# Nyström attention with two expert layers on one core: the second head group is placed in reversed partition order, eight heads' products go to the matrix array in one run, and G is made batch by batch

## The chip, the cores and the metric

The kernel runs on one core of a Trainium2 chip. Its engines work side by side, each through its own list of instructions in order: TensorE (matrix products; PE in the rows, with PEld for its weight loads), VectorE (DVE), ScalarE (ACT), GpSimd (POOL) and SyncE (SP), which here only starts DMA transfers. The metric is the device time of the whole kernel in microseconds (us), lower is better.

## The reference, cut to what matters

```
A = sm(q, k_lm);  Bm = sm(q_lm, k_lm);  C = sm(q_lm, k)     # 8 batches, 8 heads, S = 576, D = 64, 32 landmarks
Z = six steps of  Z = 2 Z - Z @ Bm @ Z                      # per head, 32 x 32
attn = A @ Z @ C @ v                                        # x = attn as (4608, 512)
x = relu(x @ w_in) ** 2 @ w_out                             # 512 -> 2048 -> 512, for every token
out = one of 8 experts for every token (relu(x @ w1) @ w2, scaled), picked by argmax(x @ w_gate)
```

All inputs are fp32. The kernel joins the end of the attention with the first layer: for each batch it makes W = Z C v (per head 32 x 64) and G = W @ w_in (32 rows of landmarks of each of 8 heads against 2048 columns), so that `x @ w_in` becomes `A @ G` with 256 rows to sum over instead of 512.

## The kernel before, in words

**Three stages.** A prologue loads q, k, v of batch 0, makes its attention parts and converts w_in and w_out. Then `gemm(b)` runs for the eight batches, each in two halves of 288 tokens (`c`): six matmuls (L998, tile `hp`) make 128 of the 2048 columns of `A @ G`, ScalarE and VectorE square them and split them into a high and a low part (L1009 to L1012), and twelve matmuls (L1045, tile `acc`) multiply by w_out, two steps later. Last, `experts` runs the expert layers (L1234, L1260).

**Side work.** While `gemm` of one batch runs, the attention of later batches is fed in small steps: `point()` is called between its matmuls and takes a share of a step (`RATE`) from `all_steps`, which weaves the `unit` of one batch with the G steps of the one before. `settle(b)` makes sure that G of batch b is there before `gemm(b)`. All of it is given to a list scheduler that fixes each engine's order when the kernel is built; a smaller priority number goes first among what it takes to be ready, and `high_priority(n)` lowers the number by n.

**Heads in the array.** The eight heads are two groups of four (`hg`), a group has its 32 landmarks of each head in 32 of the 128 partitions: head h in `32*h`. So scores (`scores_a`, `scores_c`) of a group and a half are four matmuls of a 64 x 32 weight tile and 288 columns, each into its own 32 partitions of one PSUM bank, and the same four column strips serve both groups. Batches 0 and 1 (`pe`) have q and k transposed by TensorE, with a half c in rows 64c to 64c+63 for all four heads; from batch 2 on VectorE transposes (`flipped`), and heads 0 and 1 lie in rows 0 to 63, heads 2 and 3 in rows 64 to 127.

**G.** W is written twice side by side with a mask (`hm`, L636), transposed, and is then block-diagonal with zeros: `wt[:, hg, p2]`, 128 rows (two heads) by 64 columns. Batch 0 makes G in `first_g_of` (L827) with w_in still in SBUF. Batches 1 to 3 make it alone (`g_alone`): 16 matmuls of 128 x 64 weights and 512 columns in fp32, two by two into the halves of a bank. Batches 4 and 5, and 6 and 7, make it together (`GROUPS`, `g_steps`): 48 matmuls of 128 x 128 weights and 512 columns in fp32r for two batches, for which ScalarE and GpSimd split each piece of w_in into two parts (L188, L191, tile `wi`). w_in comes back from DRAM (`win_d`) each time, in 16 pieces of 256 KB. A result goes from its bank by a ScalarE copy to `gs` and by DMA to `g_d`, from which `load_g` fetches it for `gemm`.

**Banks.** After the first G, side work has one pool of three PSUM banks (`aux`) for everything it makes; `hp` has one, `acc` four.

## Time and profile before

| | |
|---|---|
| time, median of 3 runs | 1343.86 us (1340.45 to 1346.6) |
| profiled execution: time, span | 1345.73 us, 1344.0 us |
| granted TensorE clock, mean | 0.977 of full |
| busy: PE, PEld, DVE, ACT, POOL | 95%, 83%, 59%, 47%, 29% |
| chain that ended last | PE 72%, DVE 13%, DMA 6%, issue 3%, ACT 3%, POOL 2% |
| DMA | 172.38 MB, mean 128 GB/s |

The span is the time from the first to the last instruction of the one execution that was profiled. Busy shares are of that span; matmuls overlap in the engine, so a run of them counts as one stretch from the first start to the last end. The chain is followed back from the last instruction, at each step to what released it.

### The profile page before, as it was taken

The numbers are of one execution on the slowest core, as the hardware profiler recorded it, in microseconds if no ns is written. First come the engines' busy times: TensorE is split into PE (matmuls) and PEld (weight loads), VectorE is DVE, ScalarE is ACT, GpSimd is POOL, SyncE is SP. The second block draws the span as 40 slices with busy tenths as digits, with TensorE's granted clock in tenths as the row PEclk, the third lists the DMA queues.
The fourth block names the chain that finished last, engine by engine and source line by source line (L and its number), as shares of the span: only waits on it lengthen the run. The fifth ranks groups of instructions, "written<-read, shape, count | busy, mean of one in ns | idle before, by whom it ended". The sixth has DMA issues, their size and how long they took to land.

```text
span 1344.0 us, 25108 instructions
## 1 busy us (share of the span) xinstructions
PE 1273.1 (95%) x9458; PEld 1111.6 (83%) x9458; DVE 787.0 (59%) x1760; ACT 628.6 (47%) x1385; POOL 383.6 (29%) x305
## 2 busy tenths in 40 slices
PE   6588999999999999999999999999999999999996
PEld 3267868688788888898989999998898888888885
DVE  7999968669769897787653433454423233233231
ACT  5576454455535557545654344444434334334231
POOL 3556222113013134313622112024323323323210
PEclk8688999999999999999999999999999999999998
DMA  9866283462723237613652112014345344353321
GB/s 325 272 202 184 84 279 100 170 199 77 228 63 108 82 119 210 179 62 95 207 144 67 42 35 67 1 54 140 100 129 152 100 141 134 98 157 93 106 91 37
DMA packets 126683, 172.38 MB, mean 128 GB/s; under 512 B 10558, under 2 KB 84062, under 8 KB 126558
## 3 DMA queue, kind: packets, MB, share of 16 engines
q1 hardware_dynamic: 126078, 170.18, 41.4%
q8 instruction: 76, 1.25, 0.4%
q10 hardware_dynamic: 384, 0.52, 0.1%
q14 instruction: 49, 0.40, 0.1%
q0 software_dynamic: 96, 0.03, 0.0%
HBM read 128.19 MB, written 42.51 MB: 127 GB/s over the span
## 4 chain that ended last, share of the span: by engine, by line
PE 72%; DVE 13%; DMA 6%; issue 3%; ACT 3%; POOL 2%; SPq 1%; DVEq 0%; POOLq 0%; ACTq 0%
PE acc L1045 22%; PE hp L1234 15%; PE y L1260 13%; PE hp L998 11%; PE bank L346 6%; PE y L1271 2%; DVE g L1010 2%; DVE gl L1012 2%; DVE sums L382 2%; DMA raw<-in_moe_w_in_dram 1%; PE pl L1072 1%; DMA g<-gs 1%; DMA gr<-g 1%; DVE x L413 1%; DMA w<-win 1%
## 5 line engine op out<-in xcount | busy, mean ns | idle before, releaser
L1045 PE MATMUL acc<-gh,wo 128*128 128x288 f32 x2048 | 456.6, 299 | 2.7 <-DVE wo L191 2.4
L1045 PEld LDWEIGHTS acc<-gh,wo 128*128 128x128 f32 x2048 | 342.9, 189 | 25.8 <-issue 16.0
L1045 PE MATMUL acc<-gl,wo 128*128 128x288 f32 x1024 | 288.8, 301 | 9.4 <-DVE gl L1012 9.0
L998 PE MATMUL hp<-ab,gb 128*128 128x288 f32 x1536 | 255.9, 302 | 1.3 <-ACT r L1009 0.5
L1010 DVE TENSOR_TENSOR g<-r 128x288 f32<-128x288 f32 x256 | 145.9, 571 | 162.8 <-ACT r L1009 162.1
L998 PEld LDWEIGHTS hp<-ab,gb 128*128 128x128 f32 x1536 | 219.0, 190 | 22.0 <-issue 6.9
L1009 ACT ACTIVATE r<-hp 128x288 f32<-128x288 f32 x256 | 105.3, 412 | 242.3 <-PE hp L998 237.8
L1234 PEld LDWEIGHTS hp<-xs,s 128*128 128x128 f32 x1536 | 210.7, 188 | 8.9 <-issue 0.9
L1234 PE MATMUL hp<-xs,s 128*128 128x288 f32 x1536 | 215.5, 295 | 0.0
L1045 PEld LDWEIGHTS acc<-gl,wo 128*128 128x128 f32 x1024 | 193.9, 189 | 21.8 <-DVE gl L1012 15.6
L1260 PE MATMUL y<-s,h 128*128 128x512 f32 x768 | 190.6, 396 | 0.0
L1260 PEld LDWEIGHTS y<-s,h 128*128 128x128 f32 x768 | 141.3, 188 | 29.2
L1012 DVE TENSOR_TENSOR gl<-g,gh 128x288 fp32r<-128x288 f32 x256 | 144.9, 566 | 25.9 <-ACT gh L1011 8.2
L191 POOL TENSOR_TENSOR s<-r,s 128x512 fp32r<-128x512 f32 x64 | 83.2, 1300 | 245.5 <-ACT s L188 241.6
L191 DVE TENSOR_TENSOR s<-r,s 128x512 fp32r<-128x512 f32 x64 | 51.5, 805 | 152.2 <-ACT s L188 152.1
L191 POOL TENSOR_TENSOR gb<-gr,gb 128x512 fp32r<-128x512 f32 x56 | 74.4, 1330 | 225.3 <-ACT gb L188 118.0
L188 ACT CAST s<-r 128x512 fp32r<-128x512 f32 x128 | 78.6, 617 | 116.2 <-PE y L1271 91.8
L1243 DVE SCALAR_TENSOR_TENSOR h<-hp,h 128x64 fp32r<-128x64 f32 (+2 forms) x192 | 62.7, 355 | 113.1 <-ACT h L1240 113.0
L1011 ACT ACTIVATE gh<-r 128x288 fp32r<-128x288 f32 x256 | 114.1, 446 | 6.6
L1240 ACT ACTIVATE h<-hp 128x288 fp32r<-128x288 f32 x128 | 52.5, 411 | 134.3 <-PE hp L1234 125.4
L382 DVE TENSOR_REDUCE sums<-t 128x32 f32<-128x576 f32 x64 | 71.2, 1165 | 10.1 <-DMA t<-in_q_dram 5.6
L191 POOL TENSOR_TENSOR xs<-xr,xs 128x1152 fp32r<-128x1152 f32 x16 | 45.7, 2862 | 68.4 <-ACT xs L188 63.2
(193 smaller groups left out, 1327.2 us busy)
## 6 DMA issues: line engine op xcount, KB each, us to landing
r<-in_moe_w_dram SPq DMA_DIRECT2D x128, 256.0 KB
w<-win SPq DMA_DIRECT2D x80, 256.0 KB
gr<-g SPq DMA_DIRECT2D x56, 256.0 KB
t<-in_k_dram SPq DMA_DIRECT2D x16, 576.0 KB
t<-in_q_dram SPq DMA_DIRECT2D x16, 576.0 KB
v<-in_v_dram SPq DMA_DIRECT2D x48, 192.0 KB
x_d<-x SPq DMA_DIRECT2D x16, 576.0 KB
xr<-x_d SPq DMA_DIRECT2D x16, 576.0 KB
```

Source lines behind the costliest of these rows:

```text
L188: hi = self.nc.scalar.copy(out=t[:, 0], in_=raw)
L191: (lo_eng or self.nc.gpsimd).tensor_tensor(out=t[:, 1], in0=raw, in1=t[:, 0].bitcast(F32), op=ALU.subtract)
L346: self.last_pe = self.nc.tensor.matmul(out, **kw)
L382: self.nc.vector.tensor_reduce(out=s[:, 0, ds], in_=t[:, :, ds].rearrange("p s d -> p d s"), axis=AX.X, op=ALU.add)
L998: mm = nc.tensor.matmul(hp[:, 0:HC], lhsT=g[:, l, hg, fs], rhs=at[:, r, hg, :], start=(i == 0), stop=(i == 5))
L1009: nc.scalar.activation(out=r, in_=hp[:, 0:HC], func=ACTF.Relu, scale=1.0 / 256)
L1010: nc.vector.tensor_tensor(out=g2, in0=r, in1=r, op=ALU.mult)
L1011: nc.scalar.activation(out=gh, in_=r, func=ACTF.Square)
L1012: nc.vector.tensor_tensor(out=gl, in0=g2, in1=gh.bitcast(F32), op=ALU.subtract)
L1045: nc.tensor.matmul(acc[m][:, 0:HC], lhsT=self.wo[f][:, l, ms], rhs=r, start=(f == 0 and i == 0), stop=(f == NFC - 1 and i == 2),)
L1234: nc.tensor.matmul(hp[:, 0:HC], lhsT=s1[:, l, kk, :], rhs=xs[j, c][:, r, kk, :], start=(k == 0), stop=(k == 3 * KD - 1),)
L1260: nc.tensor.matmul(acc[t], lhsT=l, rhs=s2[:, r, :], start=(first and k == 0), stop=(last and k == 2))
```

## The change: what it does

1. `place_of`: in the second head group head h lies in partitions `32*(3-h)`, everywhere (scores, softmax B, C v, W, G). A head of the first group and one of the second that share the 64 rows of the array then stand in different column strips.
2. From batch 2 on `scores` issues both groups of a half: eight matmuls into two banks, the second group first, at a priority raised by 300 (`TOGETHER`). Batches 0 and 1 keep four at a time.
3. W is no longer masked: it is written twice by the last addition itself (`hm` and L636 go), and after the transpose each head's 64 x 32 weights stand twice, in rows 0 to 63 and 64 to 127.
4. G is made for one batch at a time, in fp32: `g_part` issues eight matmuls of 64 x 32 weights and 512 columns for 512 of the 2048 columns, into two banks, with the same raised priority. So 32 matmuls of a batch stand where 16 (128 x 64, fp32) or 24 (128 x 128, fp32r) stood. The splits of w_in (L188 and L191 with `wi`) and the low part of W (L662) go.
5. w_in is kept in `win_d` as four pieces of 1 MB and fetched by 28 DMAs of 1 MB (before: 80 of 256 KB); two pieces are held, and piece n + 2 is fetched once the matmuls on n are done. G is stored by DMAs of 512 KB (before 256 KB, or 128 KB).

```diff
-GROUPS = [(0,), (1,), (2,), (3,), (4, 5), (6, 7)]
+LAST = 6
+TOGETHER = 300
...
+def place_of(hg, h):
+    i = 3 - h if hg else h
+    return slice(32 * i, 32 * i + 32)
...
-    def scores_a(self, u, hg, c):
...
-        sa = self.bank()
-        for h in range(4):
-            p, x = self.columns(u, "q", hg, h, c)
-            self.matmul(sa[32 * h:32 * h + 32, 0:HC], lhsT=u["kl"][p, hg, h, :], rhs=x, start=True, stop=True)
...
+    def scores(self, u, lm, nm, groups, c):
+        banks = {hg: self.bank() for hg in groups}
+        with self.tc.high_priority(TOGETHER):
+            for hg, h in itertools.product(reversed(groups), range(4)):
+                p, x = self.columns(u, nm, hg, h, c)
+                self.matmul(
+                    banks[hg][place_of(hg, h), 0:HC], lhsT=u[lm + "l"][p, hg, h, :], rhs=x, start=True, stop=True
+                )
+        return banks
+
+    def parts_of(self, u):
+        return [((hg,), c) for hg in range(2) for c in range(2)] if u["pe"] else [((0, 1), c) for c in range(2)]
...
+        if i == 6:
+            wb = u["wb"] = sm.tile([128, 2, 2, D], F32, tag="ks", name="wb", bufs=1)
+            twice = [128, 2, 2, D]
+            nc.vector.tensor_tensor(
+                out=wb, in0=was[:, :, LM:].unsqueeze(2).to_broadcast(twice),
+                in1=pp[:, :, LM:].unsqueeze(2).to_broadcast(twice), op=ALU.add,
+            )
+            return
...
+        u["wt"] = self.wtp.tile([128, 2, 128], F32, tag="wt", name="wt", bufs=2)
+        nc.scalar.copy(out=u["wt"].rearrange("p g x -> p (g x)"), in_=pw[:, 0:256])
...
+    def g_part(self, wt, w):
+        pg = [self.bank(), self.bank()]
+        with self.tc.high_priority(TOGETHER):
+            for hg, h in itertools.product((1, 0), range(4)):
+                p, at = slice(64 * (h % 2), 64 * (h % 2) + 64), place_of(hg, h)
+                self.matmul(pg[hg][at], lhsT=wt[p, hg, at], rhs=w[2 * hg + h // 2][p], start=True, stop=True)
+        return pg
...
+    def g_steps(self, u):
...
+        def fetch(n):
+            if n < 4:
+                raws[n] = self.wi.tile([128, KD, 512], F32, tag="wi", name="w")
+                nc.sync.dma_start(out=raws[n], in_=self.win_d[n])
+
+        for n in range(2):
+            fetch(n)
+        for _ in range(4):
             yield STEP
...
+        for n in range(4):
+            w = raws.pop(n)
+            pg = self.g_part(u["wt"], [w[:, k] for k in range(KD)])
+            fetch(n + 2)
+            gs = self.gs.tile([128, 2, 512], F32, tag="gs", name="gs")
+            for hg in range(2):
+                nc.scalar.copy(out=gs[:, hg], in_=pg[hg])
+            self.put_g(u["b"], n, gs)
+            for _ in range(4):
                 yield STEP
```

What the scheduler makes of it, at the places that the prediction speaks of. First TensorE at G of batch 2, before (a row is a run of like instructions; `w,wt` are G's matmuls):

```order
L346 MATMUL bank<-w,wt_2917 64x512 x6
L998 MATMUL hp<-ab,gb 128x288 x6
L1045 MATMUL acc<-gh,wo 128x288 x4
L349 MATMUL bank<-ident,sums 128x128 x2
L1045 MATMUL acc<-gl,wo 128x288
```

and with the change, the same place and, 22 rows on, the third piece of w_in:

```order
L349 MATMUL bank<-w,wt 32x512 x12
L935 MATMUL hp<-ab,gb 128x288 x6
L982 MATMUL acc<-gh,wo 128x288 x4
L349 MATMUL bank<-w,wt 32x512 x4
L982 MATMUL acc<-gl,wo 128x288
```
```order
L982 MATMUL acc<-gh,wo 128x288
L349 MATMUL bank<-x,lm 32x288 x8
L349 MATMUL bank<-w,wt 32x512 x4
L935 MATMUL hp<-ab,gb 128x288 x6
L982 MATMUL acc<-gh,wo 128x288
```

Before, pairs of G matmuls stood in runs of two, four or six; now the eight of a piece stand in one run where both banks were free in the schedule (the first run of twelve is piece 0 and half of piece 1), and otherwise as two runs of four. Over batches 1 to 7 these 224 matmuls make 45 sets that can stand in the array at once (7 runs of eight, 4 runs of twelve that are a set of eight and one of four, 30 sets of four or what a shorter run breaks off).

Second, TensorE at the second kind of scores (`scores_a`) of batch 2 with the change (`x,lm` are the scores' matmuls), where the first half's two groups stand apart and the second half's eight together:

```order
L982 MATMUL acc<-gh,wo 128x288
L349 MATMUL bank<-x,lm 32x288 x4
L349 MATMUL bank<-bc,dg 128x96
L935 MATMUL hp<-ab,gb 128x288 x6
L982 MATMUL acc<-gh,wo 128x288 x4
```
```order
L982 MATMUL acc<-gh,wo 128x288
L349 MATMUL bank<-eu,dg 128x96
L349 MATMUL bank<-x,lm 32x288 x8
L349 MATMUL bank<-eu,dg 128x96
L935 MATMUL hp<-ab,gb 128x288 x6
```

Before, batches 2 to 7 have 48 groups of four there; with the change 16 runs of eight and 16 groups of four.

Third, SyncE's list at G of batch 2 with the change (`win_108` is w_in's third piece, `win_109` the fourth, `win_106` and `win_107` the first two, for the next batch):

```order
L367 DMA t<-in_q_dram 128x1152
L367 DMA t<-in_k_dram 128x1152
L860 DMA w<-win_108 128x2048
L848 DMA g_0_134<-gs 128x1024
L860 DMA w<-win_109 128x2048
L848 DMA g_1_135<-gs 128x1024
L882 DMA gr<-g_0_134 128x2x256 x2
L860 DMA w<-win_106 128x2048
```

The first two pieces of a batch are fetched a batch ahead; the third and the fourth are fetched while the first two are used, behind two loads of q and k.

## Rows read from the trace of the kernel before

**Rows 1.** Busy time of the engines in stretches of the span: stretch (us), its length, then busy us (and instructions) of PE, PEld, DVE, ACT and POOL, the granted TensorE clock, the DMA engines' share and GB/s.

```profile
50.00:62.00 12.00, 8.05 (x42) 3.39 (x42) 11.82 (x18) 7.35 (x15) 8.49 (x9) 0.62 0.91 294
205.00:266.00 61.00, 59.00 (x465) 47.83 (x465) 46.11 (x106) 26.73 (x62) 12.88 (x13) 1.00 0.38 121
430.00:483.00 53.00, 52.85 (x523) 47.07 (x522) 47.13 (x125) 28.83 (x71) 9.39 (x9) 1.00 0.23 69
483.00:547.00 64.00, 61.10 (x478) 53.10 (x477) 49.65 (x89) 41.13 (x93) 29.27 (x26) 1.00 0.68 202
648.00:704.00 56.00, 54.26 (x374) 50.17 (x373) 31.34 (x67) 31.81 (x71) 22.80 (x17) 1.00 0.59 169
744.00:912.00 168.00, 167.18 (x1217) 157.74 (x1216) 74.73 (x185) 68.93 (x159) 25.62 (x18) 1.00 0.14 41
912.00:1344.00 432.00, 419.45 (x2478) 373.21 (x2476) 135.43 (x312) 153.84 (x294) 120.22 (x77) 0.99 0.39 114
```

**Rows 2.** Groups of TensorE's matmuls by form, for scores (`x,lm`) and G (the other three): busy us, mean ns of one record, then the idle time ahead of them and what ended it. An fp32 matmul leaves two records, an fp32r one leaves one.

```profile
L346 PE MATMUL bank<-x,lm 64*32 64x288 f32 x512 | 46.0, 442 | 2.7 <-DVE gb L837 1.3 <-ACT gs L934 0.9 <-ACT lm L447 0.5
L346 PE MATMUL bank<-wi,wt 128*128 128x512 f32 x96 | 28.7, 404 | 1.3 <-ACT wi L188 1.0 <-DVE wt L662 0.3
L346 PE MATMUL bank<-w,wt 128*64 128x512 f32 x96 | 28.4, 614 | 1.3 <-DMA w<-win 1.3
L827 PE MATMUL bank<-wf,wt 128*64 128x512 f32 x32 | 10.8, 797 | 1.1 <-ACT wt L660 0.6 <-ACT x L398 0.4
```

**Rows 3.** Scores in TensorE's order of time (start us, length us, records): one group of four heads of batch 3, and three groups in a row of batch 5, each with the row behind it.

```profile
260.97 0.69 PE L346 MATMUL bank<-x,lm 64*32 64x288 f32 x8
261.59 0.40 PE L1045 MATMUL acc<-gl,wo 128*128 128x288 f32 x1
...
434.96 1.66 PE L346 MATMUL bank<-x,lm 64*32 64x288 f32 x24
436.55 0.40 PE L1045 MATMUL acc<-gh,wo 128*128 128x288 f32 x1
```

**Rows 4.** The scores' records alone in two stretches of the same length, with the records that started in them: stretch, length, PE busy us (records), granted clock, DMA share and GB/s. The first is of batch 1, two groups behind each other that read rows 0 to 63 and rows 64 to 127; the second is of batch 5.

```profile
86.10:86.56 0.46, 0.42 (x16) 1.00 0.31 125
434.90:435.36 0.46, 0.40 (x8) 1.00 0.00 0
```

**Rows 5.** The run of batch 1 of which rows 4 show a part, in order of time.

```profile
86.14 0.72 PE L346 MATMUL bank<-x,lm 64*32 64x288 f32 x16
```

**Rows 6.** G of batches 1 to 3 in order of time: a set of two matmuls (batch 3) and a run of six (batch 2), each with the row behind it.

```profile
343.02 1.08 PE L346 MATMUL bank<-w,wt 128*64 128x512 f32 x4
344.03 0.44 PE L349 MATMUL bank<-ident,sums 128*128 128x128 f32 x2
...
246.78 2.80 PE L346 MATMUL bank<-w,wt 128*64 128x512 f32 x12
249.51 1.06 PE L998 MATMUL hp<-ab,gb 128*128 128x288 f32 x6
```

**Rows 7.** G of batches 6 and 7 in order of time: a run of nine matmuls and the row behind it.

```profile
656.74 2.26 PE L346 MATMUL bank<-wi,wt 128*128 128x512 f32 x9
658.84 0.96 PE L998 MATMUL hp<-ab,gb 128*128 128x288 f32 x6
```

**Rows 8.** Waits at G, in order of time: in brackets the idle us ahead of the row and what ended it.

```profile
254.95 1.04 PE L346 MATMUL bank<-w,wt 128*64 128x512 f32 x2 [1.34 <-DMA w<-win]
514.20 0.69 PE L346 MATMUL bank<-x,lm 64*32 64x288 f32 x8 [0.92 <-ACT gs L934]
687.96 0.50 PE L346 MATMUL bank<-wi,wt 128*128 128x512 f32 x1 [1.04 <-ACT wi L188]
```

**Rows 9.** The chain that ended last, at G of batch 2 (start us, us, what): 512 KB of w_in in two DMAs.

```profile
248.80 6.02 DMA w<-win
254.81 0.14 issue
```

**Rows 10.** The engines in the stretch of rows 9, columns as in rows 1.

```profile
249.00:262.00 13.00, 11.52 (x72) 8.01 (x68) 7.17 (x12) 4.94 (x12) 0.80 (x2) 1.00 0.92 325
```

**Rows 11.** The first G (batch 0) in order of time, and what follows it.

```profile
55.26 5.56 PE L827 MATMUL bank<-wf,wt 128*64 128x512 f32 x16 [0.55 <-ACT wt L660]
60.75 0.55 PE L349 MATMUL bank<-ident,t 128*128 128x128 f32 x3
```

**Rows 12.** Groups on VectorE, ScalarE and GpSimd that the change removes or touches (columns as in rows 2).

```profile
L636 DVE TENSOR_TENSOR wb<-eu,hm 128x256 f32<-128x256 f32 x8 | 3.3, 416 | 0.1
L662 DVE TENSOR_TENSOR wt<-bank,wt 128x256 fp32r<-128x256 f32 x4 | 1.7, 421 | 0.9 <-ACT wt L660 0.9
L837 DVE TENSOR_TENSOR gb<-bank,gb 128x256 fp32r<-128x256 f32 x16 | 6.2, 412 | 0.7 <-ACT gb L834 0.7
L461 DVE STREAM_TRANSPOSE aa<-bank 128x288 f32<-128x288 f32 x32 | 15.1, 472 | 3.0 <-PE bank L346 2.9
L188 ACT CAST wi<-w 128x512 fp32r<-128x512 f32 x32 | 19.6, 620 | 3.1 <-DMA w<-win 2.8 <-POOL wi L191 0.3
L934 ACT COPY gs<-bank 128x512 f32<-128x512 f32 x32 | 18.7, 584 | 16.7 <-DMA g<-gs 12.9 <-PE bank L346 3.3
L191 POOL TENSOR_TENSOR wi<-w,wi 128x512 fp32r<-128x512 f32 x32 | 42.8, 1346 | 35.7 <-ACT wi L188 31.7 <-PE bank L346 3.9
```

More of the change, by code (lines that the diff above doesn't have):

```diff
@@ L204, in job @@
                 place,
[L205 removed]
+                lambda w: self.nc.sync.dma_start(out=self.win_d[n][:, kp], in_=w),
             )
@@ L280, in run @@
             stage = self.experts(jobs)
-            for b in GROUPS[-1]:
+            for b in range(LAST, B):
                 self.gemm(b, last=stage)
@@ L302, in constants @@
         make_identity(nc, ident)
-        self.win_d = {
-            (n, k): drm.tile([128, 512], F32, name=f"win_{n}_{k}") for n in range(4) for k in range(KD)
-        }
+        self.win_d = [drm.tile([128, KD, 512], F32, name=f"win_{n}") for n in range(4)]
         self.at_d = [[drm.tile([128, S], F32, name=f"at_{b}_{g}") for g in range(2)] for b in range(B)]
@@ L478, in softmax_a, with scores_c @@
         yield STEP
-    def scores_c(self, u, hg, c):
+    def scores_c(self, u, groups, c):
         nc = self.nc
-        if hg == c == 0:
+        if groups[0] == c == 0:
             u["mc"] = self.sm.tile([128, 2, 8], F32, tag="mc", name="mc")
             u["ec"] = self.wk.tile([128, 2, S], F32, tag="ec", name="ec")
-        sc = self.bank()
-        for h in range(4):
-            p, x = self.columns(u, "k", hg, h, c)
-            self.matmul(sc[32 * h:32 * h + 32, 0:HC], lhsT=u["ql"][p, hg, h, :], rhs=x, start=True, stop=True)
-        to, src = u["ec"][:, hg], sc[:, 0:HC]
-        if u["pe"]:
-            to = to.rearrange("p (r c i l) -> p c i r l", c=2, i=3, l=LM)[:, c]
-            src = src.rearrange("p (i r l) -> p i r l", i=3, l=LM)
-        else:
-            to = to[:, c * HC:(c + 1) * HC]
-        nc.scalar.copy(out=to, in_=src)
-        nc.vector.tensor_reduce(out=u["mc"][:, hg, c:c + 1], in_=sc[:, 0:HC], axis=AX.X, op=ALU.max)
-        if c == 1:
+        for hg, sc in self.scores(u, "q", "k", groups, c).items():
+            to, src = u["ec"][:, hg], sc[:, 0:HC]
+            if u["pe"]:
+                to = to.rearrange("p (r c i l) -> p c i r l", c=2, i=3, l=LM)[:, c]
+                src = src.rearrange("p (i r l) -> p i r l", i=3, l=LM)
+            else:
+                to = to[:, c * HC:(c + 1) * HC]
+            nc.scalar.copy(out=to, in_=src)
+            nc.vector.tensor_reduce(out=u["mc"][:, hg, c:c + 1], in_=sc[:, 0:HC], axis=AX.X, op=ALU.max)
+        for hg in groups if c == 1 else ():
             mc, ec = u["mc"][:, hg], u["ec"][:, hg]
@@ L699, in unit @@
             yield STEP
-        for hg in range(2):
-            for c in range(2):
-                self.scores_c(u, hg, c)
-                yield STEP
+        for hg, c in self.parts_of(u):
+            self.scores_c(u, hg, c)
+            yield STEP
         def cv():
@@ L756, in sooner, with unit_of @@
             yield STEP
-    def unit_of(self, b, bi, wt, early=None):
-        return dict(b=b, bi=bi, wt=wt, early=early, pe=b < PE_BATCHES)
-    def weights_of(self, parts):
-        made = []
-        def get():
-            if not made:
-                made.extend(
-                    self.wtp.tile([128, 2, 2, 2, 64], F32R if parts == 2 else F32, tag=f"wt{j}", name=f"wt{j}")
-                    for j in range(parts)
-                )
-            return made
-        return get
+    def unit_of(self, b, early=None):
+        return dict(b=b, early=early, pe=b < PE_BATCHES)
     def prologue(self, right):
@@ L839, in all_steps @@
     def all_steps(self):
         g = iter(())
-        for group in GROUPS[1:]:
-            wt = self.weights_of(len(group))
-            for bi, b in enumerate(group):
-                yield from weave(self.unit(self.unit_of(b, bi, wt)), g)
-            g = self.g_steps(group, wt)
-        yield from g
-    def put_g(self, group, hg, n, gs, rows):
-        def store():
-            for bi, b in enumerate(group):
-                self.nc.sync.dma_start(
-                    out=self.g_d[b][n][rows, hg, :], in_=gs[64 * bi:64 * bi + 64] if len(group) == 2 else gs
-                )
-        self.after(2, store)
-        if hg == 1 and rows.stop == 128:
-            self.after(3, lambda: self.have.update((b, n) for b in group))
```

138 lines of the change are left out of this document (29 added, 109 removed).

## The prediction

> **What bounds the kernel now.** I read the stretches first. From 205 us on TensorE is busy nearly all the time (59.0 of 61 us, 52.85 of 53, 61.1 of 64, 167.2 of 168), at the full clock [rows 1]. So a microsecond taken off TensorE's work between about 150 and 704 us is worth a microsecond, as long as nothing else comes up behind it. What could is VectorE: 47.1 of 53 us at 430 to 483 [rows 1]. Before 62 us it is the other way round: VectorE is busy 11.8 of 12 us, TensorE 8.1, at a clock of 0.62. From 744 us on there is no side work, and the change has nothing there: 600 of the 1344 us stay.
>
> Next the groups by form: scores and G are what the change touches [rows 2]. Then their places in order of time, for what one set takes away from `gemm`: the distance from its start to the start of the next matmul, since the last record is drawn out beyond that.
>
> **Scores.** A group of four takes 0.62 us (260.97 to 261.59), and three in a row take 1.59 [rows 3], so 0.49 for a further one: a set on its own pays some 0.13 us for going to the small tiles and back. Do eight stand side by side? Batch 1 shows it without the change: two groups behind each other, one on rows 0 to 63 and one on rows 64 to 127, in the same four column strips and in two banks. In 0.46 us 16 records start, where in batch 5 only eight do [rows 4], and the whole run of 16 is drawn 0.72 us long against 0.69 for eight [rows 5, 3]. So eight cost 0.65 us instead of 0.62 + 0.62 apart. The order shows that only 16 of the 24 pairs came to stand together. Before: 48 x 0.62 less two runs of three (0.26 each) = 29.2 us. After: 16 x 0.65 + 16 x 0.62 = 20.3 us. That is **-8.9 us**.
>
> The Trainium skill ("TensorEngine Tiling (Array Packing)", Restrictions and Gotchas) says that different row tiles cannot use the same PSUM bank at the same time. By that, a group of four with heads in both row halves of one bank would go in two turns, and every set of the new G, which has both halves in each bank, too. The trace disagrees for sets in different partitions of the bank: batch 5 has its heads 0 and 1 in the upper and 2 and 3 in the lower rows, in one bank, and its eight records start within 0.46 us [rows 4].
>
> **G.** Before, batches 1 to 3: a set of two matmuls takes 1.01 us, three sets 2.73 [rows 6]; the group's 28.4 us [rows 2] less the 0.07 by which the last record of each of its 24 runs is drawn out (1.08 against 1.01) gives 26.7. Batches 4 to 7: nine fp32r matmuls take 2.10 us, 0.233 each [rows 7], times 96 = 22.4. Together 49.1 us. After, no row shows four or eight matmuls of 64 x 32 with 512 columns. A set streams the same 512 columns as the sets of two, in fp32, and four or eight narrow scores took no longer than fewer of them, so I take 1.01 for four, 1.05 for eight, 1.9 for twelve. The bounds: at best 0.85 (a further set in the run of six: (2.73 - 1.01)/2), at worst the eight go as two fours, 1.9. The 45 sets of the order: 30 x 1.01 + 7 x 1.05 + 4 x 1.9 = 45.3, less 0.13 for the ten that stand right beside scores = 44.0 us: **-5.1 us**. Had all 28 eights come together it would be 29, -20 us; the two banks that were not free in the schedule cost most of what G could give.
>
> **The old waits at G.** 1.34 for w_in, 0.92 for a bank whose `gs` copy was late, 1.04 for a split [rows 8]. The places are gone in this form: **-3.3 us**. The copies, which waited 12.9 us for their stores [rows 12], remain.
>
> **New waits for w_in.** Piece 2 of a batch is fetched when piece 0 has been used. Between the two stand, in batch 2, 12 `hp` and 24 `acc` matmuls at 0.138 each (168 us for 1217 [rows 1]), half of piece 1, four small transposes and one run of scores: 5.0 + 1.0 + 0.4 + 0.65 = 7.1 us. By the same count it is 7 to 8 us in batches 1, 2, 4, 6 and 7, 11 in batch 5 and 16 in batch 3; piece 3 has 16 to 20 (6 in batch 7). Now 512 KB took 6.0 us from issue to use at that very place [rows 9], where the DMA engines were busy 0.92 and moved 325 GB/s [rows 10]. Another 512 KB is 1.6 us more: 7.6. With one more load of q or k (576 KB, 1.8 us) ahead it is 9.4. So a wait of 0 to 2.3 us in five batches; the nearest row is itself a wait, so I take 1 us in each: **+5 us**. TensorE is in order: all of `gemm` stands behind that wait. Bounds 0 and +12.
>
> **Two banks at once.** A run of eight needs two of the three banks free when it comes up; what is behind it on TensorE waits too. Emptying one is 0.47 us on VectorE or 0.58 on ScalarE [rows 12]. All the waits ahead of scores and G sum to 5.3 us now [rows 2], mostly named above. Below: nothing. Above: half of the 52 places (24 pairs of scores, 28 pieces of G) wait for one copy, 26 x 0.5 = 13. Nearest to what is there: **+2 us**.
>
> **The first G.** 16 records took 5.5 us (55.26 to 60.75) at the low clock [rows 11]. As two sets of eight they would take 3.5. But behind them are the copies and 16 subtractions of 0.41 us [rows 12] on a VectorE that is nearly full there [rows 1]. Bounds 0 and -2, I take **-1 us**.
>
> **Costed at nothing.** The mask (L636, 8 x 0.42) and the low part (L662, 4 x 0.42) lie on VectorE beside `gemm`; the splits of w_in are 19.6 us of ScalarE and 42.8 of GpSimd [rows 12]. The stretches with the splits, less the 11 us of G in each, are no longer than others, so they hardly delay TensorE; were the cover gone, a split that TensorE waits for is 1 us [rows 8]. 28 MB of w_in instead of 20 MB is 26 us of DMA at 325 GB/s, in stretches where the DMA engines are mostly idle; it shows only as the wait priced above. G by batch also lets batch 4's G come before unit 5; `gemm(4)` has no wait of its own in the rows.
>
> **Sum.** The profiled execution took 1345.7 us. -8.9 -5.1 -3.3 +5 +2 -1 = -11.3 gives 1334.4. It stands 1.9 above the median of the runs, so the median should come to **1332.5 us**, call it 1332.
>
> **Rivals.**
> *More comes out (about 1319).* Pieces land in time, banks are free, the first G counts in full: +5 and +2 become 0, -1 becomes -2, and without splits and with fewer changes of tile size some 5 us of other waits go too. For it: GpSimd and ScalarE lose 62 us in the stretches where `gemm` runs slowest (64 and 56 us). Against: the DMA was full at G.
> *The waits take the gain (about 1342).* w_in +9, banks +7 instead of 5 and 2: 1332.5 + 9. For it: the raised priority puts each set at the first moment that the schedule thinks possible, so whatever is later in fact is a wait of TensorE.
> *Slower (about 1355).* The 1 MB pieces. If loads of q, k and w_in and the stores of G queue up so that the 14 pieces 2 and 3 are waited for 2 us each on the mean, in place of 5 us in all: 1332.5 - 5 + 28. It decides from 1.2 us a piece on (then the time is that of before), and from 1.7 us it is half a percent slower. For it: 0.92 busy [rows 10]; against: mean use is 69 to 202 GB/s [rows 1], and piece 3 has 16 us.
> *Eight do not stand together with 512 columns, or only as fours.* Then each eight of G costs 1.9: 11 x 0.85 = +9, about 1342; rows 4 speak against it.
> *By the rule on row tiles and banks*, each set of G would go in two turns: 45 x 0.85 = +38, and scores would not gain: about 1379. Rows 4 show the opposite for 288 columns.
>
> **Chances.** Forecast (1325 to 1337) 0.50, more 0.18, waits 0.18, no eights 0.04, slower 0.08, the rule 0.02. Half a percent is 6.7 us, about what a measurement of this kernel can tell: faster (under 1337) 0.68, same 0.23, slower 0.09. The range takes in the better rival and the waits: 1317 to 1346.
>
> **What would show it.** Right: `x,lm` records in runs of 16 drawn about 0.7 us long; `w,wt` runs of eight records about 1.08 us and of 16 about 1.1, under a name with 64 rows by 32 columns; their busy sum near 48 against 57.1 us; `gemm(6)`, which starts the stretch at 744, about 11 us earlier; from there on the same 600 us. Waits for `w<-win` ahead of piece 2, around 1 us. Wrong: G records in two turns (1.9 us for 16); idle time of TensorE behind `gs` copies or `w<-win` above 10 us in sum; VectorE at over 95% of a stretch while TensorE idles; or a start of `gemm(0)` that moved by several us, since the order of the prologue moved too.

## The result, and the profile after

The changed kernel takes 1364.38 us (median of 4 runs, 1357.15 to 1366.31) against 1343.6 for the kernel before in the same session: a ratio of 1.0148, 95% interval 1.0115 to 1.0181. It is slower by 21 us where 11 us of gain were forecast. The profiled execution took 1364.93 us with a span of 1363.2 and a mean clock of 0.963.

**The priced terms held.** TensorE's groups by form, columns as in [rows 2]:

```profile
L982 PE MATMUL acc<-gh,wo 128*128 128x288 f32 x2048 | 466.0, 303 | 5.2 <-ACT wo L196 2.7 <-ACT gh L948 2.1 <-DVE wo L199 0.3
L982 PE MATMUL acc<-gl,wo 128*128 128x288 f32 x1024 | 294.9, 304 | 16.0 <-DVE gl L949 15.7
L935 PE MATMUL hp<-ab,gb 128*128 128x288 f32 x1536 | 262.7, 307 | 13.6 <-ACT r L946 9.1 <-DVE gb L826 4.4
L349 PE MATMUL bank<-w,wt 64*32 64x512 f32 x448 | 48.1, 600 | 3.1 <-DMA w<-win 3.1
L349 PE MATMUL bank<-x,lm 64*32 64x288 f32 x512 | 37.1, 445 | 2.3 <-ACT et L587 1.3 <-DVE mc L512 0.5 <-ACT lm L450 0.5
```

Scores went from 46.0 to 37.1 us, G from 28.7 + 28.4 to 48.1, and the waits for w_in are 3.1 us. What is new stands in the other three groups, which are `gemm`'s own: TensorE waits 9.1 us for `r` and 15.7 for `gl`. The same two groups before:

```profile
L1045 PE MATMUL acc<-gl,wo 128*128 128x288 f32 x1024 | 288.8, 301 | 9.4 <-DVE gl L1012 9.0
L998 PE MATMUL hp<-ab,gb 128*128 128x288 f32 x1536 | 255.9, 302 | 1.3 <-ACT r L1009 0.5 <-DVE gb L837 0.5
```

The sets took what was forecast (1.01, 1.05 and 1.9). In order of time, a set of four matmuls of G (8 records), one of eight (16) and a run of twelve (24), each with the row behind it, answering [rows 6]:

```profile
259.85 1.06 PE L349 MATMUL bank<-w,wt 64*32 64x512 f32 x8
260.84 0.40 PE L982 MATMUL acc<-gl,wo 128*128 128x288 f32 x1
...
524.05 1.09 PE L349 MATMUL bank<-w,wt 64*32 64x512 f32 x16
525.07 0.69 PE L1009 MATMUL pl<-x,wg 128*32 128x288 f32 x8
...
256.48 1.92 PE L349 MATMUL bank<-w,wt 64*32 64x512 f32 x24
258.33 1.06 PE L935 MATMUL hp<-ab,gb 128*128 128x288 f32 x6
```

From start to start they take 0.99, 1.02 and 1.85 us.

**Where the time went.** The stretch from 205 to 640 us, first before and then after, columns as in [rows 1]:

```profile
205.00:640.00 435.00, 425.44 (x3692) 366.51 (x3692) 343.80 (x797) 228.93 (x533) 112.10 (x105) 1.00 0.42 129
```
```profile
205.00:640.00 435.00, 412.40 (x3618) 347.88 (x3615) 320.97 (x746) 213.88 (x501) 78.60 (x76) 0.96 0.47 150
```

TensorE, VectorE, ScalarE and GpSimd are all less busy, and the clock is lower: they have less to do and wait for each other (and a stretch of fixed length holds a little less of the work of the longer kernel). To split the loss I took the distances between the starts of neighbouring matmul records from the first `hp` of `gemm(0)` to the first of `gemm(6)`: *beside* is the distances with a side matmul at one end or both; *waits* are distances between two matmuls of `gemm` above 0.43 us, less the 0.13 that a matmul takes at the full clock; *slow* is the same for 0.19 to 0.43 us; *low clock* is the time at a granted 0.50, which is 1.2 GHz. The ratio is to the kernel before in the same session.

| kernel | median us | ratio (95%) | beside | waits | slow | low clock |
|---|---|---|---|---|---|---|
| before | 1343.6 | | 218.8 | 11.6 | 22.9 | 17.1 |
| after | 1364.38 | 1.0148 (1.0115 to 1.0181) | 204.1 | 32.9 | 37.6 | 51.2 |
| e1, scores singly, G new | 1351.75 | 1.0072 (1.0046 to 1.0097) | 207.2 | 22.2 | 28.4 | 20.5 |
| e2, no raised priority | 1363.42 | 1.0147 (1.0117 to 1.0176) | 213.4 | 30.0 | 36.9 | 44.4 |
| e3, scores in pairs, G old | 1383.24 | 1.0306 (1.0278 to 1.0334) | 211.1 | 42.6 | 32.4 | 34.1 |
| e4, follow-up in two steps | 1365.16 | 1.0164 (1.0139 to 1.0188) | 203.8 | 32.6 | 39.5 | 51.2 |
| e5, flips behind `gl` | 1353.65 | 1.007 (1.0052 to 1.0087) | 212.1 | 23.0 | 28.6 | 23.9 |
| e8, pairs twice | 1390.61 | 1.0356 (1.0337 to 1.0375) | 233.6 | 29.9 | 33.8 | 44.4 |
| e9, after at 0.58 | 1365.06 | 1.0141 (1.0112 to 1.017) | 203.6 | 36.8 | 39.3 | 54.6 |
| e11, after at 0.52 | 1381.96 | 1.0279 (1.0252 to 1.0307) | 223.7 | 33.5 | 36.9 | 44.4 |
| e13, `gl` on GpSimd | 1351.12 | 1.0051 (1.0031 to 1.0071) | 205.2 | 24.2 | 30.1 | 27.3 |
| e14, `scores_a` singly | 1350.0 | 1.0055 (1.0038 to 1.0072) | 207.0 | 23.6 | 29.6 | 27.3 |
| e15, `scores_c` singly | 1355.35 | 1.0079 (1.005 to 1.0108) | 193.6 | 34.5 | 32.5 | 34.1 |
| e16, `g` on ScalarE | 1360.0 | 1.012 (1.0095 to 1.0144) | 211.8 | 23.5 | 27.4 | 23.9 |
| e17, e13 and e14 | 1352.13 | 1.0063 (1.0043 to 1.0084) | 214.5 | 18.7 | 29.6 | 27.6 |
| e18, no flips on VectorE | 1352.39 | 1.0071 (1.0049 to 1.0093) | 212.4 | 21.6 | 28.2 | 28.4 |
| e5b, before with e5's edit | 1366.83 | 1.0165 (1.0143 to 1.0187) | 229.5 | 16.1 | 29.3 | 34.1 |
| e10, before at 0.66 | 1350.8 | 1.0049 (1.003 to 1.0067) | 222.9 | 12.2 | 25.8 | 20.5 |
| e12, before at 0.58 | 1353.98 | 1.0068 (1.0043 to 1.0093) | 221.2 | 16.6 | 24.2 | 17.1 |
| e13b, before, `gl` on GpSimd | 1349.59 | 1.0042 (1.0025 to 1.0059) | 227.2 | 6.8 | 25.5 | 17.1 |

After less before: 14.7 us less beside `gemm`, 21.3 us more waits and 14.7 us more slow matmuls, together +21.3; `gemm(0)` starts 1.0 us earlier, and from the start of `gemm(6)` to TensorE's last matmul both take 587.0 us. The loss arises later: `gemm(1)` starts at 205.16 us, still 0.6 us earlier than before, and from there `gemm(1)` to `gemm(5)` take 12.9 and 7.3 us more, 3.0 less, 9.1 more and 6.2 less. Of the new waits 15.8 us lie between 205 and 640 us. (The last four columns go by the one profiled execution. For e2 it took 1372.09 us and for e16 1353.37, 9 above and 7 below the median; the others are within 6 us.)

**The stalls.** Behind the last `scores_a` of batches 2 to 6, from some 5 to 13 us after it, TensorE stalls: it is idle 13.1 of the 75 us that five stretches of 15 us from there make up. One of these stalls is that of batch 3, whose run starts at 303.47: VectorE in order of time after the change (in brackets the idle us ahead of a row and what ended it),

```profile
304.23 0.48 DVE L479 STREAM_TRANSPOSE aa<-bank 128x288 f32<-128x288 f32 x1 [1.89 <-PE bank L349]
304.63 1.39 DVE L416 STREAM_TRANSPOSE x<-t 128x576 f32<-128x576 f32 x2
305.95 0.71 DVE L486 TENSOR_REDUCE ma<-aa 128x18 f32<-128x576 f32 x1
306.58 0.47 DVE L479 STREAM_TRANSPOSE aa<-bank 128x288 f32<-128x288 f32 x1
306.98 1.39 DVE L416 STREAM_TRANSPOSE x<-t 128x576 f32<-128x576 f32 x2
308.30 0.39 DVE L663 TENSOR_TENSOR dg<-bank,h 128x256 f32<-128x256 f32 x1
308.61 1.46 DVE L947 TENSOR_TENSOR g<-r 128x288 f32<-128x288 f32 x1
310.10 0.77 DVE L416 STREAM_TRANSPOSE x<-t 32x576 f32<-32x576 f32 x1
310.90 0.75 DVE L486 TENSOR_REDUCE ma<-aa 128x18 f32<-128x576 f32 x1
311.68 0.77 DVE L416 STREAM_TRANSPOSE x<-t 32x576 f32<-32x576 f32 x1
312.48 0.75 DVE L492 TENSOR_REDUCE ma<-aa 128x18 f32<-128x576 f32 x1
313.15 1.42 DVE L947 TENSOR_TENSOR g<-r 128x288 f32<-128x288 f32 x1
314.50 1.51 DVE L949 TENSOR_TENSOR gl<-g,gh 128x288 fp32r<-128x288 f32 x1
```

the `r` that ScalarE makes there, what TensorE waits for,

```profile
308.90 0.39 ACT L946 ACTIVATE r<-hp 128x288 f32<-128x288 f32 x1
309.34 1.06 PE L935 MATMUL hp<-ab,gb 128*128 128x288 f32 x6 [0.60 <-ACT r L946]
312.30 1.70 PE L935 MATMUL hp<-ab,gb 128*128 128x288 f32 x6 [1.91 <-ACT r L946]
316.06 0.61 PE L982 MATMUL acc<-gl,wo 128*128 128x288 f32 x1 [2.06 <-DVE gl L949]
```

and the stretch as a whole, then the stretch at the low clock that begins in it, and one behind the stall of batch 5:

```profile
303.00:318.00 15.00, 10.27 (x71) 8.67 (x70) 13.55 (x20) 8.40 (x17) 6.40 (x5) 0.81 0.18 51
312.40:319.20 6.80, 4.74 (x19) 4.39 (x20) 6.68 (x11) 2.27 (x5) 3.29 (x3) 0.50 0.30 82
493.40:500.20 6.80, 6.14 (x24) 5.79 (x25) 6.51 (x14) 2.33 (x6) 1.46 (x2) 0.50 0.11 34
```

VectorE is busy 13.55 of 15 us while TensorE is busy 10.27. From 304.23 to 308.61 it runs only side work: two `aa`, four flips (`x<-t`, of the next batch's k), a maximum and a `dg`. The `g` at 313.15 has had its `r` since 309.29 and stands behind two more flips, a maximum and a sum; its `gl` ends at 316.01, and TensorE starts again at 316.06. `r` and `g` have two buffers each, so ScalarE can't run far ahead of a late `g`; the waits for `r` are likely of the same origin. From 312.40 to 319.20 TensorE runs at 0.50. Before the change the same work of the same batch alternates with `g` and `gl`:

```profile
305.28 1.67 DVE L1010 TENSOR_TENSOR g<-r 128x288 f32<-128x288 f32 x1
306.98 0.77 DVE L413 STREAM_TRANSPOSE x<-t 32x576 f32<-32x576 f32 x1
307.78 0.50 DVE L1012 TENSOR_TENSOR gl<-g,gh 128x288 fp32r<-128x288 f32 x1
308.32 0.78 DVE L413 STREAM_TRANSPOSE x<-t 32x576 f32<-32x576 f32 x1
309.12 0.62 DVE L1010 TENSOR_TENSOR g<-r 128x288 f32<-128x288 f32 x1
```

Over 200 to 640 us VectorE ran 26.7 us of flips of q and k before, and 42.2 after, while a `g` or `gl` had its inputs. Counted once for each `g` or `gl` that stood behind them, as below, it is 29.2 and 64.6 us.

Two places fit this and are not proof: the smallest of the stalls, that of batch 6 (1.4 of 15 us idle), stands behind two groups of four that came apart, and batch 7, whose last `scores_a` are a run of eight, has no stall behind it and no later batch whose flips could come.

### The profile page after: what moved, and what is told of

It is laid out like the page before. It is cut to its first block, busy times and chain, and to the rows that moved or that the text cites. A ratio compares the mean times of both kernels' runs of the same rounds, so it can differ in the third digit from the quotient of the medians.

```text
span 1363.2 us, 25397 instructions
## 1 busy us (share of the span) xinstructions
PE 1278.5 (94%) x9746; PEld 1107.5 (81%) x9746; DVE 770.7 (57%) x1743; ACT 612.4 (45%) x1353; POOL 334.9 (25%) x273
## 4 chain that ended last, share of the span: by engine, by line
PE 77%; DVE 13%; DMA 5%; issue 2%; ACT 1%; POOL 0%; SPq 0%; DVEq 0%; ACTq 0%
PE acc L982 26%; PE hp L1171 15%; PE y L1197 13%; PE hp L935 12%; PE bank L349 6%; DMA w<-win 2%; PE y L1208 2%; DVE sums L385 2%; DVE x L416 2%; DVE g L947 2%; DVE x L420 1%; PE pl L1009 1%; DVE m L171 1%; DVE m L172 1%; DMA t<-in_q_dram 1%
## 5 line engine op out<-in xcount | busy, mean ns | idle before, releaser
L982 PE MATMUL acc<-gh,wo 128*128 128x288 f32 x2048 | 466.0, 303 | 5.2 <-ACT wo L196 2.7
L982 PEld LDWEIGHTS acc<-gh,wo 128*128 128x128 f32 x2048 | 347.5, 192 | 29.8 <-issue 15.1
L982 PE MATMUL acc<-gl,wo 128*128 128x288 f32 x1024 | 294.9, 304 | 16.0 <-DVE gl L949 15.7
L935 PE MATMUL hp<-ab,gb 128*128 128x288 f32 x1536 | 262.7, 307 | 13.6 <-ACT r L946 9.1
L935 PEld LDWEIGHTS hp<-ab,gb 128*128 128x128 f32 x1536 | 222.9, 194 | 36.5 <-ACT r L946 14.0
L947 DVE TENSOR_TENSOR g<-r 128x288 f32<-128x288 f32 x256 | 134.1, 524 | 169.3 <-ACT r L946 168.8
L1197 PEld LDWEIGHTS y<-s,h 128*128 128x128 f32 x768 | 141.0, 188 | 29.5
L949 DVE TENSOR_TENSOR gl<-g,gh 128x288 fp32r<-128x288 f32 x256 | 132.6, 518 | 22.2 <-ACT gh L948 2.2
L948 ACT ACTIVATE gh<-r 128x288 fp32r<-128x288 f32 x256 | 113.9, 445 | 22.7 <-PE acc L982 12.1
L385 DVE TENSOR_REDUCE sums<-t 128x32 f32<-128x576 f32 x64 | 71.1, 1165 | 15.8 <-DMA t<-in_q_dram 10.1
```

The source lines that it names most:

```text
L385: self.nc.vector.tensor_reduce(out=s[:, 0, ds], in_=t[:, :, ds].rearrange("p s d -> p d s"), axis=AX.X, op=ALU.add)
L935: mm = nc.tensor.matmul(hp[:, 0:HC], lhsT=g[:, l, hg, fs], rhs=at[:, r, hg, :], start=(i == 0), stop=(i == 5))
L947: nc.vector.tensor_tensor(out=g2, in0=r, in1=r, op=ALU.mult)
L948: nc.scalar.activation(out=gh, in_=r, func=ACTF.Square)
L949: nc.vector.tensor_tensor(out=gl, in0=g2, in1=gh.bitcast(F32), op=ALU.subtract)
L982: nc.tensor.matmul(acc[m][:, 0:HC], lhsT=self.wo[f][:, l, ms], rhs=r, start=(f == 0 and i == 0), stop=(f == NFC - 1 and i == 2),)
```

## The experiments

First the change was taken apart: e1 keeps the new G and issues every group of scores by itself; e3 is the kernel before with reversed places and pairs of scores; e2 takes the raised priority away; e4 puts the second group's follow-up one step later.

```diff
 # e1
-        return [((hg,), c) for hg in range(2) for c in range(2)] if u["pe"] else [((0, 1), c) for c in range(2)]
+        return [((hg,), c) for hg in range(2) for c in range(2)]
 # e2
-TOGETHER = 300
+TOGETHER = 0
 # e3, against before; scores_a and scores_c call scores as in the change, G and its splits stay
+def place_of(hg, h):
+    i = 3 - h if hg else h
+    return slice(32 * i, 32 * i + 32)
+    def scores(self, u, lm, nm, groups, c):
...
 # e4, in scores_a and scores_c
+            if hg == 0 and len(groups) == 2:
+                yield STEP
```

e1: 

> One part undone: scores come group by group again (four heads, one bank, a step of its own for each), at the raised priority; the reversed places and G by batch stay. The changed kernel took 1364, the kernel before 1343.6. Theory A (the pairs of scores are the cause: both groups' follow-up work on VectorE and ScalarE comes in one burst, ahead of what gemm needs, TensorE waits and its clock falls): the bursts go, the 9 us that pairs save on TensorE go too, 1335 to 1342, and idle of hp before ACT r falls from 9.1 to under 2 us. Theory B (G by batch is the cause: late 1 MB loads, two banks at once): 1360 to 1372, hp still waits about 9 us. Theory C (the raised priority): little change, 1360 to 1370. Theory D (any change of the order costs or gains some ten us by chance): anywhere between 1335 and 1370, with waits at other places.

e2: 

> One number changed: TOGETHER is 0 instead of 300, so scores and G stand in the schedule at their own place in the program, and fewer sets of eight stay whole. Theory C (the raised priority brings scores and G too early, and TensorE waits in order): 1335 to 1345. Theories A and B: 1360 to 1370, as the steps and their follow-up work are the same. Theory D: anywhere between.

e3: 

> The kernel before with only the scores changed: reversed places in the second group, pairs of groups in two banks at the raised priority; G as before (mask, batches 1 to 3 alone, 4 and 5 and 6 and 7 together). Theory A: the bursts come with the pairs, so 1355 to 1368, hp waits for ACT r for 5 us or more. Theory B: 1333 to 1338, the 9 us less on TensorE come out. Theory C: 1355 to 1368 as A, since the scores are raised here too. Theory D: anywhere between.

e4: 

> The changed kernel with one edit: the eight matmuls of a pair of scores stay in one call, but the follow-up work of the second group comes one step after that of the first, so a unit has its 51 steps again instead of 47. Theory A, if the burst comes from fewer steps: the time falls to 1340 to 1350 and hp's wait for ACT r halves. Theories B and C: 1358 to 1368. If the burst comes from the two groups becoming ready together, whatever the steps: 1358 to 1368 as well.

Measured: 1351.75, 1363.42, 1383.24 and 1365.16. Each against the kernel before in its own session, the change costs 20.8 us and e1 10.1: pairs cost some 11 us beside the new G, and some 40 beside the old (e3), although the time beside `gemm` gets shorter both times (by 3 and 8 us). The new G alone costs 10 us. Neither the priority nor the number of steps makes a difference that can be told.

**Is it VectorE's order?** e5 and e5b hold the flips of q and k and the two row reductions of `softmax_a` in VectorE's order behind the last `gl` that was emitted (`follow` adds an order, no wait); the flips of the scores, which the expectation names too, are left free. e8 issues each matmul of a pair twice. e10 is the kernel before with only the order disturbed.

```diff
 # e5 on the changed kernel, e5b on the one before
+    def yields(self, ins):
+        if len(self.gls) >= 1:
+            self.follow(ins, self.gls[-1])
...
+            self.yields(ins)
 # e8
-                self.matmul(
-                    banks[hg][place_of(hg, h), 0:HC], lhsT=u[lm + "l"][p, hg, h, :], rhs=x, start=True, stop=True
-                )
+                for _ in range(len(groups)):
+                    self.matmul(
+                        banks[hg][place_of(hg, h), 0:HC], lhsT=u[lm + "l"][p, hg, h, :], rhs=x, start=True, stop=True
+                    )
 # e10, against before
-RATE = 0.65
+RATE = 0.66
```

e5: 

> The changed kernel, with one kind of side work on VectorE (the 32 x 32 flips of the next batch's q and k and of the scores, and the two reductions of the mask row) held in VectorE's order behind the last subtraction gl of the gemm step that was emitted before it. Nothing is left out; no work is added. Theory F (side work stands on VectorE in a burst ahead of gemm's own g and gl, TensorE waits for these and then runs at the low clock): waits inside gemm(0) to gemm(5) fall from 33 us to 15 or less, low-clock time from 51 us to 20 or less, and the time to 1332 to 1345. Theory D (any other order moves the time by about 10 us either way, without a common cause): the time moves, but waits of acc<-gl and hp<-r do not fall together; anything from 1350 to 1375. If TensorE's low clock came from its own activity and not from the waits: waits fall, low-clock time stays near 50 us, about 1355.

e5b: 

> The same rule for VectorE's order put into the kernel before. Theory F: the kernel before has few of these bursts (waits in gemm 11.6 us), so it changes little: 1335 to 1345. If the rule is good or bad by itself, whatever the pairs do, it moves here by as much as it moves the changed kernel.

e8: 

> The changed kernel with each matmul of the scores issued twice where both groups are issued together (batches 2 to 7), into the same place and with the same result: 24 sets more of eight. TensorE's own work grows by 24 x about 0.5 = 12 us. If only what TensorE has to do counts: 1364 + 12 = 1376. Theory F (the order on VectorE and ScalarE follows from what the schedule believes of TensorE): the order shifts again, and waits and low-clock time change by more than the added work, to 1385 or more, or to less than 1370. If TensorE has slack in these stretches behind the stalls, the added work is hidden: 1364 to 1368.

e10: 

> The kernel before with side work fed at 0.66 steps a point in place of 0.65: the same work, a little earlier. It measures how far the time moves when only the order moves. Theory D: 5 to 15 us off 1342 either way. Theory F: within 4 us, since the groups of scores still come one by one.

Measured: 1353.65, 1366.83, 1390.61 and 1350.8. The same rule gains some 10 us after the change and loses 24 before it. In e5 waits and low clock fall, the waits by half of what was expected (to 23.0 us, not 15); some groups fall apart (beside +8), so it isn't a clean cure. In e8 the added matmuls cost more than the 12 us I gave them (beside +29.5, and no run shows why), and waits and low clock stayed near where they were: a longer run of scores, which moves the whole order, doesn't remove them. And e10 was a surprise: the same work, fed 1.5% faster, costs 8 us.

**Is it the density?** With pairs a batch has fewer steps, so at one rate its work comes earlier.

```diff
 # e9 (e11: 0.52) on the changed kernel, e12 on the one before
-RATE = 0.65
+RATE = 0.58
```

e9: 

> The changed kernel with side work fed at 0.58 steps a point in place of 0.65, all else as it is. With the change a batch has fewer steps in its attention part (two groups' scores are one step), and in the trace each batch's last scores stand 0.25 to 0.45 of a half of gemm earlier than before, counted in hp matmuls: the same work on VectorE and ScalarE is packed into less gemm. Theory P (this density is what makes g, gl and r late): waits inside gemm(0) to gemm(5) fall from 33 us to 20 or less, low-clock time from 51 to 30 or less, 1335 to 1350. Theory O (it is the order inside a step, whatever the density): waits stay at 28 to 38 us, 1358 to 1370. Theory D (chance of the order): no link between the time and the density.

e11: 

> The changed kernel at 0.52 steps a point, a fifth thinner. Theory P: at least as good as at 0.58 as long as G is ready for its gemm in time, 1330 to 1345. If the work left over is then forced in a block ahead of a gemm that needs its G, halves of gemm get long at the batch boundaries: 1350 to 1375. Theory O: 1358 to 1370.

e12: 

> The kernel before at 0.58 steps a point in place of 0.65, the control: it has 11.6 us of waits inside gemm, of which a thinner feed could take a few. Theory P: 1335 to 1345. Theory D, after 0.66 cost 8 us: 1345 to 1360.

Measured: 1365.06, 1381.96 and 1353.98. The density theory falls: waits stay at 33 to 37 us. (At 0.52 the time beside `gemm` grows by 20 us besides.) The kernel before loses 10 us at this rate also, so its 0.65 is better than either neighbour.

**Which pairs, and which queue?** e13 and e13b move `gl` to GpSimd; e14 issues only `scores_a` singly, e15 only `scores_c`.

```diff
 # e13 on the changed kernel, e13b on the one before
-                nc.vector.tensor_tensor(out=gl, in0=g2, in1=gh.bitcast(F32), op=ALU.subtract)
+                (nc.gpsimd if b < LAST else nc.vector).tensor_tensor(
+                    out=gl, in0=g2, in1=gh.bitcast(F32), op=ALU.subtract
+                )
 # e14 (e15: the other way round)
-            for hg, c in self.parts_of(u):
+            for hg, c in self.parts_of(u, True):
                 self.scores_a(u, hg, c)
```

e13: 

> The changed kernel with gemm's subtraction gl (the last step ahead of TensorE's acc) on GpSimd instead of VectorE in gemm(0) to gemm(5). GpSimd is busy only 25% of the span. Nothing is left out. Theory Q (gl stands in VectorE's queue behind side work): acc<-gl waits fall from 15.7 us, with them hp<-r and the low clock; waits inside gemm 33 to 15 or less, time 1335 to 1350. If the subtraction is much slower there, or GpSimd's own side work takes VectorE's place, new waits for gl come in place of the old: 1355 to 1375. If the waits have nothing to do with VectorE's queue: 1360 to 1368.

e13b: 

> The same in the kernel before. Theory Q: 11.6 us of waits can at most be won, and GpSimd is also splitting w_in there: 1335 to 1355, the changed kernel gains 10 us or more beyond this one. If gl on GpSimd is good or bad by itself, both move by the same amount.

e14: 

> The changed kernel with the second kind of scores (scores_a) one group after the other, each a step of its own, as before; the first kind (scores_c) stays in pairs. Theory Q, with the burst behind the last scores of a batch (when both groups' buffers of q come free at once and the next batch's flips start): the stalls 4 to 12 us behind them go, waits 33 to about 22, 1348 to 1356. If it is the pairs of the first kind: 1360 to 1366.

e15: 

> The other half: scores_c one group after the other, scores_a in pairs. Theory Q: the stalls stay, 1358 to 1366. If it is the pairs of the first kind: waits fall to about 22 us, 1346 to 1356.

Measured: 1351.12, 1349.59, 1350.0 and 1355.35. Moving `gl` gains some 14 us after the change and loses 5 before it; the waits fall to 24.2 us, where 15 or less was expected. With `scores_a` single the waits fall to 23.6 (47.1 us of flips ahead of `g` and `gl`); with `scores_c` single they stay (34.5, and 69.5 us of flips ahead of `g` and `gl`), and its 9 us come from beside `gemm`. So the waits that pairs bring hang on those of `scores_a`.

**How far does it go?** e16 computes `g` on ScalarE, e17 joins e13 and e14, e18 takes the flips off VectorE.

```diff
 # e16
+                if b < LAST:
+                    nc.scalar.activation(out=g2, in_=r, func=ACTF.Square)
+                else:
+                    nc.vector.tensor_tensor(out=g2, in0=r, in1=r, op=ALU.mult)
 # e18
-                self.nc.vector.transpose(
+                self.nc.gpsimd.tensor_copy(
```

e16: 

> The changed kernel with gemm's fp32 square g computed by ScalarE instead of VectorE in gemm(0) to gemm(5); gl stays on VectorE. It takes some 190 x 0.52 = 100 us off VectorE and adds some 190 x 0.45 = 85 us to ScalarE, which is less busy there. Theory Q, if load on VectorE is what counts: waits inside gemm 33 to 20 or less, 1340 to 1352. If ScalarE's queue (r, gh, now g, with the copies of the flipped x among them) takes its place: hp<-ACT r waits grow above the 9.1 us, 1360 to 1380.

e17: 

> The changed kernel with scores_a one group after the other (alone 1350) and gl on GpSimd (alone 1351). If the two cures remove different waits: 1364 - 14 - 13 = 1337, below the time of before. If they remove the same waits: 1346 to 1351, and what is left over 1343 is not in VectorE's queue.

e18: 

> The changed kernel with the flips of q and k of batches 2 to 7 replaced by plain copies of the same size on GpSimd: the 32 x 32 blocks are not transposed, so this part of the computation is left out, and VectorE is rid of 24 x 4 instructions (some 70 us) that stood in front of g and gl. All else stays, pairs and G by batch too. If the flips are the whole cause: waits inside gemm fall from 33 us to that of before (12) or less, low clock to 20, and TensorE's 18 us come out: 1328 to 1340. If they are one of several things in VectorE's queue (sums, row maxima): waits near 23, 1346 to 1353. If VectorE's queue is not it: 1358 to 1368. GpSimd's copies may be late for scores; that shows as waits of scores, not of gemm.

Measured: 1360.0, 1352.13 and 1352.39. In e16 TensorE's waits for `r` fall from 9.1 to 3.0 us, but those for `gl` only from 15.7 to 14.0, and beside `gemm` 7.7 us come on top: it gains about 4 us, and neither of its two theories holds. The two cures of e17 remove the same loss. In e18 the stalls behind `scores_a` of batches 3 to 5 are gone: the 15 us that begin with those runs, columns as in [rows 1]:

```profile
295.00:310.00 15.00, 14.37 (x120) 13.44 (x119) 12.51 (x21) 9.59 (x21) 12.52 (x14) 1.00 0.20 56
376.00:391.00 15.00, 14.38 (x120) 13.45 (x119) 12.28 (x26) 9.25 (x22) 7.83 (x10) 1.00 0.12 40
472.00:487.00 15.00, 14.38 (x119) 13.42 (x118) 12.64 (x23) 9.20 (x20) 9.43 (x11) 1.00 0.07 21
```

TensorE is busy 14.4 of 15 us at the full clock, against 10.27 at 0.81 for batch 3. Over batches 2 to 6 it is idle 2.8 of the 75 us, against 13.1. What TensorE waited for from 205 to 640 us, after the change (us in sum, times, longest) and in e18:

```profile
PE hp L935 <- ACT r L946: 9.1, 10, 1.9
PE acc L982 <- DVE gl L949: 5.3, 6, 2.1
PE acc L982 <- ACT gh L948: 2.1, 5, 1.0
```
```profile
PE acc L982 <- DVE gl L949: 7.8, 8, 2.4
PE hp L935 <- ACT r L946: 1.9, 3, 1.2
```

Waits inside `gemm` in that stretch, counted as in the table, are 4.6 us before, 20.4 after, 11.2 in e14 and 9.1 in e18. Taking the flips off VectorE thus removes some 11 of the 16 us more. It isn't all: e18 keeps 9 us, its two longest waits (2.4 and 2.1 us) at other places than the stalls above, and the time beside `gemm` is 8 us longer, where some groups fell apart.

**What is shown and what stays open.** Shown: pairs of `scores_a` bring the stalls (e14, e15), the stalls are VectorE's side work, the flips above all, ahead of `g` and `gl` (the rows above, e5, e13, e18), and low clock follows most of them. A likely reason for the queue, argued only: the q of both groups is released by one run, so the next batch's flips of both groups, which take over its buffers, become ready together. More buffers would tell; this wasn't tried. Open: why no cure goes below 1350. That is also where the kernel before lands when its order is disturbed (e10, e12 and e13b: 1350 to 1354; e5b is worse), so its 1343 belongs to one order; and what TensorE saves in e1 or e14 (beside -12 us) comes back as waits (+10.6 and +12.0) and slow matmuls (+5.5 and +6.7). No single place stands out for those, so a third of the new waits between 205 and 640 us (5.8 of 15.8, which e1 has too) has no shown cause; the reversed places and the 1 MB pieces were not run by themselves. No version here beats the kernel before.

## Why the prediction was wrong

**The sum.** Scores: forecast -8.9, and their busy time fell by 8.9. That the two agree is luck: 1.8 us of the fall lie in batches 0 and 1, and only 12 of the 24 pairs stand in one run, where 16 were counted (in four more a set of G stands between the two groups). G: forecast near 48 us of busy time, measured 48.1. By the prediction's own measure, from the start of a run to the next other matmul, scores and G of batches 1 to 7 (scores from batch 2 on) together fell by 15.2 us with the waits inside left out, where 14.0 was forecast. So these two terms held. The old waits at G are gone, as forecast. New waits for w_in: 3.1 us where 5 was taken; the four pieces that TensorE waited for took 7.0 to 9.2 us from issue to use, near the estimate, and the other 24 landed in time. Two pieces in the chain that ended last, and one of the four waits:

```profile
258.77 7.90 DMA w<-win
...
612.10 9.19 DMA w<-win
```
```profile
182.45 1.06 PE L349 MATMUL bank<-w,wt 64*32 64x512 f32 x8 [0.86 <-DMA w<-win]
```

Two banks: all of the 2.3 us of idle time ahead of scores lies before 103 us, where scores still go four at a time, and ahead of G only w_in is waited for; nothing, where 2 was taken. The first G: `gemm(0)` starts 1.0 us earlier, as forecast, but then waits 4.40 us for a `gb` of that G, where it waited 0.5 before; by `gemm(1)` the two kernels are level within 0.6 us.

```profile
64.94 1.33 PE L935 MATMUL hp<-ab,gb 128*128 128x288 f32 x4 [4.40 <-DVE gb L826]
```

The stretch from `gemm(6)` on is the same, as forecast.

**The step that failed** is the first paragraph's condition, and "Costed at nothing". I wrote that a microsecond off TensorE is worth one "as long as nothing else comes up behind it", named VectorE at 47.1 of 53 us [rows 1], and then priced only the instructions that the change adds or removes on it. What the change moves there got no price: eight heads' scores in one run set two groups' follow-ups and the next batch's flips ready at about the same time, VectorE runs them in the order of the list, and `g` and `gl`, on which TensorE's next matmuls hang, stand behind them. (That the flips stand there is shown by the rows above; that they come ready together is argued.) In all `gemm` got +21.3 us of waits and +14.7 of slow matmuls, terms that the sum has at nothing. Between 205 and 640 us, where the loss arises, the waits are 4.6 us before, 10.4 in e1 and 20.4 after, the slow matmuls 13.9, 17.6 and 26.0: two thirds of both come with the pairs. The other third is there in e1 too, with single groups, the new G and another order, and its cause stays open. Busy shares could not show the queue: VectorE's busy time fell, from 787.0 to 770.7 us of the whole span. Its order at the places where pairs come to stand might have.

**The rivals.** "The waits take the gain" was the right kind, but with w_in and the banks it named the wrong waits. "Slower" decided on the 1 MB pieces, which were in time. The Trainium skill's rule on row tiles that share a bank ("TensorEngine Tiling (Array Packing)", Restrictions and Gotchas) was given 1379, by G in two turns; the trace disagrees, since a set of eight with both row halves in each bank took 1.02 us, so the kernel is slower for another reason. Of the signs that I gave for wrong, the one on VectorE comes nearest, and its mark of 95% was too high: the stall shown has 13.55 of 15 us, and only that of batch 2 passes the mark (14.46 of the 15 us from 217.2).

## What to carry to other kernels

Where in-order engines hand a product round (here TensorE, ScalarE, VectorE, TensorE), merging two pieces of side work can also merge their follow-ups; ask what will stand in the next engine's list ahead of the critical chain, and price that queue, not only the instructions saved. Before crediting a gain to less work, disturb the order of the old kernel without changing its work: here 1.5% on a rate moved it by 8 us, as much as the largest term of the sum.
